# Attention units tied to MLP steps, in a fused attention and ELU-MLP kernel

## The chip, the cores and the metric

One Trainium2 chip, one core. The metric is the device time of one execution in microseconds (us), lower is better. The span of a profile is about 1.8 us shorter than the time of the same execution. A run is classed slow when it is over 1.5% above the fastest of its kernel in its job; ratios use the other runs, called fast, alone. TensorE is called PE in the profile, VectorE DVE, ScalarE ACT, GpSimd POOL, and SP is the engine that issues stores and transposes; PEld is TensorE's weight load.

## The reference, cut to what matters

```python
batch, n_heads, seq, head_dim = (8, 8, 576, 64)      # q, k, v: [8, 8, 576, 64]
q_s = softmax(q over head_dim)                       # exp, divided by its sum
k_s = softmax(k over seq)
kv  = einsum('bhsd,bhse->bhde', k_s, v)              # 64 x 64 per head
att = einsum('bhsd,bhde->bhse', q_s, kv)
x   = att.transpose(0, 2, 1, 3).reshape(4608, 512)
h   = x @ w_in                                       # 512 -> 2048
g   = where(h > 0, h, exp(min(h, 0)) - 1)
out = g @ w_out                                      # 2048 -> 512
```

## The kernel before: the parts that matter

The work is cut in two ways. Attention comes in 16 *units*, each four heads of one batch. The MLP comes in 9 *blocks* of 512 tokens, each of 8 *steps*; a step makes 256 of the 2048 hidden columns. Steps are numbered through: step 8j + g is step g of block j. A program of operations with their reads and writes is built first; a planner then gives each engine its order, by estimated durations, and sets the semaphores. So the order on the chip is fixed beforehand, but each instruction still waits for the real event (in the trace before, VectorE stood 12.6 us at QS, in six waits).

One step (the clamp and the GT tile on VectorE come after each group of eight matmuls):

```python
    def hg(self, j, g, ps, key, how):
        ...   # 8 matmuls 128x128 by 128x512 into the PSUM pair PS[ps]            (line 539)
        ...   # ACT: esb = exp(PS)                                                (line 547)
        # how == "d":
            S.add("dve", ..., e.tensor_scalar(esb, esb, 1.0, -1.0, ALU.min, ALU.add) ...)    # the clamp, line 564
            S.add("dve", ..., e.tensor_tensor(gt, esb, P, ALU.max) ...)                      # GT tile, line 566
        # how == "a": ACT does relu(1 - esb), VectorE one scalar_tensor_tensor (line 560)
```

The attention chain of a unit from 6 on: exp on ScalarE, then sum, reciprocal and QS on VectorE, a transpose by DMA, a widening on GpSimd, the product on TensorE.

```python
        S.add("dve", ..., e.tensor_tensor(qso, q, rz, ALU.mult) ..., W=[f"QS{self.alt(n)}"])   # line 383
    def turn(self, n, key):
        self.S.add("sp", ..., e.dma_start_transpose(self.QT, qs) ..., R=[QS], W=["QT"], dma="tq")
        self.S.ops[-1].packet = 512
    def widen(self, n, key):
        self.S.add("gp", 1200, e.tensor_copy(T, self.QT) ..., R=["QT"], W=[qsT])
```

QS, QT and qsT have one copy each for these units. The planner takes the next operation of an engine that could start first by its estimate. How late a load or transpose is taken to land is set by `margin`:

```python
        S.ops[-1].margin = 300 if n < 4 else self.MARGIN      # MARGIN = 1500 ns; the transposes: 0
        ...
                if x[1] < 1:
                    land[x[2]] = t + 200 + x[2].margin
```

Attention is put into the program as early as its ring of X tiles allows:

```python
        for n in range(4, NU):
            ...
            steps.append([ao(n, 0, merged)] + (more if merged else []))
            steps.append([ao(n, 1)] + ([wide(n + 1)] if nxt else []) + ... +
                         ([first(n + 2), loads(("v", n + 3))] if n + 2 < NU else []))
        def piece(blocks):
            if self.pi < len(steps) and (steps[self.pi][0][0] // 2 + 1) * S_ - RING <= blocks * BLK:
                ...
```

Here `first` is the softmax (and transpose) of a unit, `wide` the widening, `kv` and `ao` its products.

The softmax here doesn't subtract the row's maximum and nothing guards it: scores larger than these inputs give would overflow.

## Time and profile before

| | before |
|---|---|
| time, the three runs at the start | 330.14, 330.22, 337.85 us |
| span of the profiled run (an execution of 328.18 us), granted clock | 326.3 us, 0.989 |
| TensorE busy | 305.5 us (94%) |
| TensorE idle between the first MLP matmul and the tail | 10.6 us |
| VectorE waiting to write QS until a transpose has read it | 12.6 us, 6 times |

How to read it: TensorE at 94% says that it is the bound on the mean, not everywhere. The idle time is length less busy time of each stretch, and the question is what ended each idle stretch. The lines are in the prediction.

### The profile page before, as it was taken

To read this page: it belongs to the slowest core of one execution; us is meant where nothing else is said; L and a number is where in the kernel's file an instruction comes from. 1 tells how busy PE (TensorE), PEld (TensorE's weight loads), DVE (VectorE), ACT (ScalarE), POOL (GpSimd) and SP (SyncE) were. 2 spreads that over 40 slices of the span, in tenths; PEclk is the share of its full clock that TensorE was granted. 3 is DMA by queue.
4 is the path that set the end of the run, shared out by engine and by line. 5 is a ranking of instruction groups with operands and counts; after the bars stand their busy time and mean duration, and the time that the engine had idled before them with its cause. 6 is when DMAs were issued, how large, how long until landed. Compare 5 with 4: busy or idle time off the path is not lost.

```text
span 326.3 us, 4708 instructions
## 1 busy us (share of the span) xinstructions
PE 305.5 (94%) x1997; PEld 239.8 (74%) x1997; DVE 196.4 (60%) x244; ACT 162.7 (50%) x190; POOL 67.2 (21%) x80
## 2 busy tenths in 40 slices
PE   6789999699799989969899999999999999999995
PEld 5577767477477767747678777877788888888873
DVE  4848656967798688376874565454455455545500
ACT  4757668783876554535545442444333333333311
POOL 0760461434453514150420011001000000000000
PEclk9999999899899999999999999999999999999999
DMA  7999998669887864977642162111111111122122
GB/s 271 308 390 390 391 390 327 162 211 169 258 293 181 221 235 93 241 210 145 228 117 57 41 70 66 27 41 32 34 32 32 35 32 32 32 49 50 32 64 65
DMA packets 29525, 49.39 MB, mean 151 GB/s; under 512 B 13888, under 2 KB 13888, under 8 KB 29504
## 3 DMA queue, kind: packets, MB, share of 16 engines
q0 software_dynamic: 10272, 33.16, 33.2%
q1 hardware_dynamic: 19232, 15.93, 21.6%
q8 instruction: 15, 0.25, 0.3%
q14 instruction: 6, 0.05, 0.1%
HBM read 36.70 MB, written 9.44 MB: 141 GB/s over the span
## 4 chain that ended last, share of the span: by engine, by line
PE 74%; DMA 14%; DVE 6%; ACT 2%; POOL 1%; SPq 1%; issue 1%
PE PS L576 35%; PE PS L539 34%; DMA QT<-QS 7%; PE PS L485 3%; DMA QR<-in_q_dram 3%; DMA VR<-in_v_dram 2%; DVE QS L383 2%; DMA W<-in_moe_w_in_dram 2%; DVE ZQ L375 1%; DVE GT L566 1%; PE PS L455 1%; DVE GT L560 1%; POOL qsT L429 1%; ACT QR L359 1%; DVE ESB L564 1%; ACT ESB L547 1%
## 5 line engine op out<-in xcount | busy, mean ns | idle before, releaser
L539 PE MATMUL PS<-XT,W 128*128 128x512 f32 x576 | 146.5, 400 | 4.0 <-DVE GT L560 2.8
L576 PE MATMUL PS<-W,GT 128*128 128x512 f32 x576 | 144.7, 394 | 2.3 <-DVE GT L566 2.3
L539 PEld LDWEIGHTS PS<-XT,W 128*128 128x128 f32 x576 | 108.2, 191 | 29.4 <-DVE GT L560 3.8
L576 PEld LDWEIGHTS PS<-W,GT 128*128 128x128 f32 x576 | 106.7, 188 | 26.6 <-DVE GT L566 3.7
L547 ACT ACTIVATE ESB<-PS 128x1024 f32<-128x1024 f32 x72 | 73.9, 1026 | 92.9 <-PE PS L539 92.9
L564 DVE TENSOR_SCALAR ESB<-ESB 128x1024 f32<-128x1024 f32 x64 | 47.4, 740 | 72.8 <-ACT ESB L547 72.3
L566 DVE TENSOR_TENSOR GT<-ESB,PS 128x1024 fp32r<-128x1024 f32 x64 | 78.2, 1221 | 2.2
L593 ACT ACTIVATE OSB<-PS 128x512 f32<-128x512 f32 x32 | 19.1, 598 | 34.2 <-PE PS L576 34.2
L383 DVE TENSOR_TENSOR QS<-QR,RZQ 128x1152 f16<-128x1152 f32 x16 | 24.1, 1509 | 13.1 <-DMA QT<-QS 12.6
L367 POOL CAST VB<-VR 128x1152 bf16<-128x1152 f32 x15 | 19.6, 1304 | 49.5 <-DMA VR<-in_v_dram 37.7
L375 DVE TENSOR_REDUCE ZQ<-QR 128x18 f32<-128x1152 f32 x16 | 21.6, 1348 | 8.3 <-ACT QR L359 8.2
L507 ACT ACTIVATE XT<-PS 128x640 fp32r<-128x640 f32 (+5 forms) x32 | 19.7, 620 | 13.6 <-PE PS L485 6.8
L359 ACT ACTIVATE QR<-QR 128x1152 f32<-128x1152 f32 x16 | 18.6, 1164 | 11.7 <-DMA QR<-in_q_dram 11.7
L429 POOL CAST qsT<-QT 128x1152 fp32r<-128x1152 f16 x10 | 11.5, 1149 | 62.3 <-PE PS L485 62.3
L485 PE MATMUL PS<-qsT,MBLK 64*128 64x320 f32 (+3 forms) x128 | 17.2, 350 | 5.0 <-DVE MBLK L467 5.0
L485 PEld LDWEIGHTS PS<-qsT,MBLK 64*128 64x128 f32 x128 | 9.7, 188 | 15.5 <-issue 7.4
L362 ACT ACTIVATE KR<-KR 128x1152 bf16<-128x1152 f32 x16 | 18.5, 1162 | 3.0 <-DMA KR<-in_k_dram 3.0
L323 POOL DMA_DIRECT2D QR<-in_q_dram x14 | 10.2, 726 | 24.6 <-DVE QS L383 22.3
L323 POOL DMA_DIRECT2D KR<-in_k_dram x14 | 10.2, 730 | 15.1 <-PE PS L455 15.1
L560 DVE SCALAR_TENSOR_TENSOR GT<-PS,ESB 128x1024 fp32r<-128x1024 f32 x8 | 9.8, 1221 | 5.0 <-ACT ESB L558 5.0
L323 POOL DMA_DIRECT2D VR<-in_v_dram x14 | 10.1, 720 | 2.4 <-POOL VB L367 2.4
L467 DVE TENSOR_SCALAR MBLK<-PS,RZK 128x64 fp32r<-128x64 f32 x32 | 9.1, 284 | 1.1
(28 smaller groups left out, 71.9 us busy)
## 6 DMA issues: line engine op xcount, KB each, us to landing
out_dram<-OSB SPq DMA_DIRECT2D x64, 128.0 KB, 2.3
QR<-in_q_dram POOLq DMA_DIRECT2D x14, 576.0 KB, 6.1
KR<-in_k_dram POOLq DMA_DIRECT2D x14, 576.0 KB, 5.2
VR<-in_v_dram POOLq DMA_DIRECT2D x14, 576.0 KB, 6.1
W<-in_moe_w_in_dram POOLq DMA_DIRECT2D x4, 1024.0 KB, 8.8
W<-in_moe_w_out_dram POOLq DMA_DIRECT2D x4, 1024.0 KB, 18.8
QR<-in_q_dram SPq DMA_DIRECT2D x2, 576.0 KB, 4.1
KR<-in_k_dram SPq DMA_DIRECT2D x2, 576.0 KB, 7.6
```

What stands on the lines that cost most here:

```text
L323: S.add(eng, ISSUE[eng], lambda e: e.dma_start(dst, src), key, W=[name], dma=f"{name}{eng}", nbytes=128 * 4608, follow=self.gpq if chain e ...
L359: S.add("act", t_act(1152, False), lambda e: e.activation(flat(q), flat(q), AF.Exp), key - 3, X=[f"qR{i}"])
L367: S.add(eng, t, lambda e: e.tensor_copy(VB[:, hs, :, 0:D], v[:, hs, :, :]), key - 50, R=[vname], W=[f"VB{i}"])
L375: S.add("dve", t_dve(1152) + 60, lambda e: e.tensor_reduce(self.ZQ[i][:, :, :].rearrange("p h c -> p (h c)"), q[:, :, :, :].rearrange("p h ...
L383: S.add("dve", t_dve(1152) + 60, lambda e: e.tensor_tensor(qso, q[:, :, :, :], rz, ALU.mult), key - 3, R=[f"qR{i}", f"RZQ{i}"], W=[f"QS{se ...
L485: last = e.matmul(P[:, h * 512:h * 512 + n_], M[hs, f, :], T[hs, c0:c1, f * 64:f * 64 + 64], start=(f == 0), stop=(f == 1))
L507: S.add("act", t_act((h1 - h0) * n_, True), lambda e, dst=dst, src=src: e.activation(dst, src, AF.Copy), key, W=W, X=X)
L539: last = e.matmul(P[:, t * 512:(t + 1) * 512], self.W1[:, kc, tt * 128:(tt + 1) * 128], self.XT[:, kc, rc:rc + BLK], start=(kc == 0), stop ...
L547: S.add("act", t_act(1024, True), lambda e: e.activation(esb[:, :], P[:, :], AF.Exp), key, W=[f"E{i}"], X=banks)
L564: S.add("dve", t_dve(1024, 2) + 80, lambda e: e.tensor_scalar(esb[:, :], esb[:, :], 1.0, -1.0, ALU.min, ALU.add), key, X=[f"E{i}"])
L566: S.add("dve", t_dve(1024) + 90, lambda e: e.tensor_tensor(gt, esb[:, :], P[:, :], ALU.max), key, R=[f"E{i}"], W=gw, X=banks)
L576: last = e.matmul(dst, GT[:, jj, ts * 128:(ts + 1) * 128], self.W2[:, jj, :], start=(jj == 0), stop=(jj == 15))
```

## The change

The intent: each stage of units 4 to 15 is tied to a given MLP step, so that the next unit's softmax is not reached while the last one's transpose still runs. An operation made under a gate may not be planned before that step's matmuls start; there is no semaphore for it. Two planning margins rise to 5000 ns. The output matmuls are taken from their list one step later. The keys by which the planner ranks attention work that could start at about the same time (`due`) follow the same table of steps. The diff is cut to these parts.

```diff
@@ one_pass: when may an operation be planned
+            if o.gate is not None:
+                if o.gate.start is None:
+                    return None
+                t = o.gate.start
@@ load, turn
-        S.ops[-1].margin = 300 if n < 4 else self.MARGIN
+        S.ops[-1].margin = 300 if n < 4 else 1500 if n < 6 else 5000
-        self.S.ops[-1].packet = 512
+        self.S.ops[-1].packet, self.S.ops[-1].margin = 512, 5000
@@ program
+        when = {n: (4 * n - 14, 4 * n - 8) for n in range(4, NU)}
+        when.update({4: (8, 9), 5: (10, 12), 6: (12, 16)})
         def due(n):
-            m = n // 2 * S_ // BLK
-            return 12 + 8 * (m - 1) - 9 + 4 * (n % 2)
+            return when[n][1] + 4 if n in when else 3 + 4 * (n % 2)
...
         for n in range(4, NU):
-            (the two steps.append of above)
+            begin, use = when[n]
+            at(begin, first(n), loads(("v", n + 1), ("q", n + 2)))
+            at(use - 2 if n >= BYDMA else use, wide(n))
+            if n == 4:
+                at(use, kv(n), loads(("k", n + 2)))
+            at(use + 1, ao(n, 0))
+            at(use + 2, ao(n, 1, n + 1 if n + 1 < NU else None), loads(("k", n + 3)))
...
+        def paced(s):
+            S.gate = self.last_hg
+            for n, go in slots.pop(s, ()):
+                go()
+            S.gate = None
@@ blocks 2 to 8
-                piece(j)
-                if work[0][0] < j:
+                paced(8 * j + g)
+                if j > 2 or g % 3:
...
+        w = work.pop()
         assert not work
+        self.out_mm(*w, key)
+        self.out_store(w[0], w[1], w[2], key + 1)
```

More of the change, by code (lines that the diff above doesn't have):

```diff
@@ L24 @@
     __slots__ = ("eng", "dur", "emit", "deps", "key", "idx", "start", "end",
-                 "dma", "sem", "val", "clock", "nbytes", "follow", "side", "late", "packet", "margin")
+                 "dma", "sem", "val", "clock", "nbytes", "follow", "side", "late", "packet", "margin",
+                 "gate")
     def __init__(self, eng, dur, emit, key, dma=None, nbytes=0):
@@ L53, in __init__ @@
         self.r = {}
+        self.gate = None
     def add(self, eng, dur, emit, key, R=(), W=(), X=(), dma=None, nbytes=0, after=(),
@@ L58, in add @@
         op.idx = len(self.ops)
-        op.follow, op.side, op.late = follow, side, False
+        op.follow, op.side, op.late, op.gate = follow, side, False, self.gate
         for d in after:
@@ L324, in load @@
               dma=f"{name}{eng}", nbytes=128 * 4608, follow=self.gpq if chain else follow)
-        S.ops[-1].margin = 300 if n < 4 else self.MARGIN
+        S.ops[-1].margin = 300 if n < 4 else 1500 if n < 6 else 5000
         if chain:
             self.gpq = S.ops[-1]
-    MARGIN = 1500
     def raw(self, t, n):
@@ L543, in hg @@
         S.add("pe", 8 * t_f32r(512), mm, key, R=xs + [f"W1_{g // 2}"], X=banks)
+        self.last_hg = S.ops[-1]
         i = self.eslot % len(self.ESB)
@@ L696, in program, with at @@
                  [first(3), loads(("v", 4)), ao(2, 0)], [ao(2, 1), wide(3)],
-                 [kv(3), loads(("q", 5), ("k", 5))], [first(4), loads(("v", 5)), ao(3, 0)],
-                 [ao(3, 1), wide(4)],
-                 [kv(4), loads(("q", 6), ("k", 6)), first(5), loads(("v", 6))]]
+                 [kv(3), loads(("q", 5), ("k", 5)), ao(3, 0)], [ao(3, 1)]]
+        slots = {}
+        def at(s, *what):
+            slots.setdefault(s, []).extend(what)
         for n in range(4, NU):
-            nxt = n + 1 if n + 1 < NU else None
-            merged = nxt if n > 4 else None
-            more = [loads(("k", n + 3), ("q", n + 3))]
-            steps.append([ao(n, 0, merged)] + (more if merged else []))
-            steps.append([ao(n, 1)] + ([wide(n + 1)] if nxt else []) +
-                         ([] if merged or not nxt else [kv(nxt)] + more) +
-                         ([first(n + 2), loads(("v", n + 3))] if n + 2 < NU else []))
-        self.pi = 0
+            begin, use = when[n]
[5 more added lines that the diff above has]
+            at(use + 2, ao(n, 1, n + 1 if n + 1 < NU else None), loads(("k", n + 3)))
         def piece(blocks):
-            if self.pi < len(steps) and (steps[self.pi][0][0] // 2 + 1) * S_ - RING <= blocks * BLK:
-                for n, go in steps[self.pi]:
-                    go()
-                self.pi += 1
+            if steps:
+                for n, go in steps.pop(0):
+                    go()
+        def paced(s):
[3 more added lines that the diff above has]
+            S.gate = None
         key = 0
-        slots = [0, 2, 1]
+        turns = [0, 2, 1]
         for g in range(8):
-            self.hg(0, g, slots[g % 3], key, "da"[g % 2])
+            self.hg(0, g, turns[g % 3], key, "da"[g % 2])
             key += 1
@@ L729, in program @@
             self.out_store(0, ts, (ts + 2) % 4, key)
-        piece(1)
+        while steps:
+            piece(1)
         for g in range(8):
             self.hg(1, g, 2 if g == 0 else g % 2, key, "da"[g % 2])
-            piece(1)
+            paced(8 + g)
             if g >= 2:
```

## The prediction

> **What bounds the kernel now.** I read the page first (busy time and the slices), then a table of busy time by stretch, the TensorE timeline, the chain of work that ended last, and the waits of each engine. From the page, the busy share and the slices of TensorE and its clock:
>
> ```profile
> PE 305.5 (94%) x1997; PEld 239.8 (74%) x1997; DVE 196.4 (60%) x244; ACT 162.7 (50%) x190; POOL 67.2 (21%) x80
> PE   6789999699799989969899999999999999999995
> PEclk9999999899899999999999999999999999999999
> ```
>
> TensorE is the bound, but not all along. From slice 20 on (163 us) it is full; before that some slices show 6 to 8, and two show a lower clock. The table by stretch (length, busy time of PE, PEld, DVE, ACT and POOL, clock, DMA share, GB/s) puts sizes on it:
>
> ```profile
> 52.00:62.70 10.70, 8.03 (x77) 5.94 (x75) 9.60 (x13) 9.34 (x11) 2.58 (x3) 1.00 0.65 205
> 62.70:71.00 8.30, 8.28 (x37) 6.36 (x38) 5.20 (x6) 5.97 (x8) 3.26 (x4) 0.79 0.63 209
> 71.00:86.00 15.00, 12.75 (x126) 9.26 (x124) 12.12 (x17) 9.97 (x12) 5.87 (x7) 1.00 0.99 222
> 107.00:119.30 12.30, 11.05 (x84) 8.47 (x82) 9.60 (x12) 7.33 (x8) 3.98 (x6) 1.00 0.89 257
> 132.50:158.20 25.70, 21.57 (x167) 16.49 (x165) 16.64 (x20) 12.46 (x15) 7.62 (x9) 1.00 0.85 188
> 158.20:190.00 31.80, 31.75 (x177) 25.18 (x178) 20.15 (x25) 14.92 (x18) 4.10 (x4) 1.00 0.34 96
> ```
>
> Length less PE busy gives TensorE's idle time: 2.67, 0.02, 2.25, 1.25, 4.13 and 0.05 us. With 0.20 us in the stretches not shown that is 10.6 us between the first MLP matmul (17.1 us) and the last. After 158 us there is none, although attention work still goes on there until 229 us. What holds TensorE up is in the chain of 132 to 160 us (start, length, what):
>
> ```profile
> 132.33 8.12 DMA QT<-QS
> 140.48 1.36 DVE QS L383
> 141.84 0.09 DVE RZK L464
> ...
> 143.55 1.17 POOL qsT L429
> ...
> 144.73 6.49 DMA QT<-QS
> ...
> 151.25 1.36 DVE QS L383
> ```
>
> and in the timelines of VectorE and TensorE at the same place:
>
> ```profile
> 140.48 1.36 DVE L383 TENSOR_TENSOR QS<-QR,RZQ 128x1152 f16<-128x1152 f32 x1 [4.15 <-DMA QT<-QS]
> 142.61 0.62 PE L485 MATMUL PS<-qsT,MBLK 64*128 64x384 f32 x4 [3.12 <-DVE MBLK L467]
> ```
>
> A unit is four heads of a batch; from unit 6 on its normalized Q (tile QS) is transposed by DMA into QT, and GpSimd widens QT to qsT. QS, QT and qsT each have one copy. With attention issued as early as possible, VectorE reaches the QS of the next unit while the DMA still reads the last one. It stands 4.15 us, and behind it stand MBLK and the MLP's own GT tiles, which TensorE needs. The attention chain (QS, transpose, widen, matmul) is then the bound, not TensorE. The same wait:
>
> ```profile
> DVE QS L383 <- DMA QT<-QS: 12.6, 6, 4.1
> ```
>
> Two groups also ran slow. The eight matmuls from 62.72 us took 3.69 us where the same eight elsewhere take 2.05 after a small attention matmul and 1.81 otherwise, so 1.64 lost; the eight from 86.08 took 3.33, so about 1.3 lost, and a little after. The clock records say the same: 8.3 us x 0.21 = 1.7, and 21 us x 0.08 = 1.7 from 86 to 107. Together 3.3 us.
>
> [...] in those 4.15 us VectorE did none of its other work. [...] the ten transposes took 2.8 to 10.2 us to land (median 4.7) for the same bytes, the long ones among Q, K and V loads. [...] half speed at 62.7 us after a stretch (58.9 to 62.7) with 1.1 us of matmuls, but none after the 3.12 us gap at 142.6.
>
> **The change part by part.** (1) No arithmetic, transfer or byte is added or removed: it is order alone. TensorE's order is the same for both kernels up to the third MLP step of block 1 (51.8 us) and in the last block. So 17.1 us of start, block 0, and 3.9 us from the last matmul to the end stay.
>
> (2) Pacing. One unit per four MLP steps from unit 8 on. A step is 8 + 8 matmuls, 3.63 us; per unit come its two products, 0.49 + 0.43, its KV product, 0.41, and about 2 x 0.24 for the slower matmuls after them: 4 x 3.63 + 1.8 = 16.3 us. The chain from softmax to QS is 1.16 + 1.35 + 0.26 + 1.36 = 4.1 us by the rows of the page's groups, some 6 with the other work of its engines; then the transpose, 4.7 at the median and 10.2 at worst; the widening, 1.15. That is 12 to 17.5 us to the widened tile, which is needed seven steps (28 us) after the beginning; and the next QS is written one period after this one, 16.3 us, more than the 10.2 of the slowest transpose. So the wait on the transpose should go, and with it the idle time at 107 to 119 and 132 to 158: 1.25 + 4.13 = 5.4 us.
>
> (3) Is VectorE able to keep TensorE full? Between two MLP tiles the changed order now puts reduce, reciprocal and QS together, 1.35 + 0.26 + 1.36 = 3.0 us. An MLP tile of VectorE normally ends about 3.2 us after its matmuls (1.03 exp, 0.74, 1.22, hops), and its PSUM tile is reused 5.4 us after them (three groups of 1.81). VectorE has about 1.5 us free in each step, so 3.0 delays a tile by about 1.5 us, less than the 2.2 us of slack. No stall, unless a GpSimd instruction coincides.
>
> (4) Block 1, steps 8 to 15, where units 4 and 5 go by TensorE transposes, and unit 6 starts. I laid the changed order out by hand from 51 us with the durations of the trace, each instruction after its engine's last one and its inputs. Now VectorE does the MLP's tile of step 9 before unit 5's softmax (before: after it, at 61.45 to 62.67), so the fourth step starts at about 59.0 and not 62.7. I then find a 0.4 us wait for MBLK and one of about 1.6 us for the copy of unit 4's first product out of PSUM, behind two MLP instructions on ScalarE (64.8 us); the second product and unit 5's KV product follow, and the fifth step at about 65.8 (before: 67.2). Then no wait up to the second step of block 2, which waits 0.8 us for VectorE and starts at 82.1, where it started at 86.08 with the same matmuls done. So 4.0 us are won there and 2.9 us of idle time stay.
>
> (5) Slow clock. [...] about 1.7 of the 3.3 us stay; I count half, 0.9. The other half was after the idle time at 84 to 86, which goes.
>
> (6) Output tiles lag one step: the last 8 matmuls of a block's outputs move into the next block's first step, and some empty places of block 2 get filled. Same count; they are further from the GT they read. At the end the final 64 output matmuls still follow the last MLP step, so nothing is gained or lost: 0.
>
> Sum: 10.6 + 3.3 = 13.9 us to be had, which would give 330.2 - 13.9 = 316.3. What I expect to stay is 0.4 + 1.6 + 0.8 + 0.9 = 3.7 us. So 330.2 - 10.2 = 320.0 us, or -3.1%.
>
> **Rivals.** A: the transposes are still late. For it: the first paced units (6 and 7) start two steps apart, about 8 us, less than the worst landing, and transposes stand on the same queue as output stores, which wait for ScalarE (159 us of waits there, mostly idle queue). Against it: the stores are now in the same regular order, and loads no longer bunch. One late transpose would cost about 2 to 4 us: 322 to 324. B: pacing pushes attention out to step 54 of 72, so XT could be late for a block's first step. By the ring and the steps, the needed part is done two to three steps ahead (unit 7 at step 21 for block 3 at 24; unit 15 at 53 for block 7 at 56). 8 us of margin speak against it; if wrong, several blocks would each lose some us, and the time is 325 to 335. C: the stalls were hidden anyway and TensorE is equally full: 328 to 331. Against: the idle time is on TensorE itself, which carries 74% of the chain. D: everything goes, 316.3.
>
> **Range and chances.** My value lies 3.7 us above the floor. 316.6 is nearly the floor; 324.2 is the value with one late transpose. 2% faster is 323.6, so I may lose up to half of the gain I count. Faster by over 2%: 0.84; within 2%: 0.14; slower: 0.02.
>
> **What would show it.** Right: the wait of QS for QT near zero; TensorE idle below 0.3 us in 107 to 160; its idle time between the first and last MLP matmul about 3 us rather than 10.6, nearly all before 85 us; attention matmuls regularly spread to some 250 us; full clock after 70 us. Step 3 is wrong if groups of 8 wait for GT in the paced part with no DMA behind it; step 4 if the second step of block 2 does not start 3 to 5 us earlier; step 5 if slow groups remain or new ones come. The whole is wrong if XT or the load of Q, K or V ends TensorE's waits.

## The result, and the profile after

The changed kernel took 319.06 us (median of 4 runs, 317.05 to 321.1) against 330.61 us before (4 runs). The ratio is 0.9655, 95% interval 0.9577 to 0.9734: faster. A ratio here is the mean time of one kernel's fast runs over that of the other's of the same rounds, so it is not quite the ratio of the medians. The predicted 320.0 is 0.9 us off.

The page of the changed kernel, the same three rows:

```profile
PE 305.3 (96%) x1997; PEld 239.8 (76%) x1997; DVE 209.2 (66%) x244; ACT 162.3 (51%) x190; POOL 67.0 (21%) x80
PE   7789999989999999999999999999999999999995
PEclk9979999999999999999999999999999999999999
```

The table by stretch, same stretches (length, busy time of PE, PEld, DVE, ACT and POOL, clock, DMA share, GB/s):

```profile
52.00:62.70 10.70, 10.53 (x54) 8.04 (x53) 8.36 (x10) 9.76 (x12) 1.86 (x2) 1.00 0.71 233
62.70:71.00 8.30, 7.10 (x109) 5.18 (x109) 7.46 (x13) 6.80 (x8) 2.93 (x4) 1.00 0.72 245
71.00:86.00 15.00, 14.72 (x102) 10.82 (x101) 12.48 (x16) 11.75 (x14) 6.30 (x7) 1.00 0.60 192
107.00:119.30 12.30, 12.30 (x57) 9.82 (x56) 8.39 (x10) 6.48 (x8) 4.49 (x5) 1.00 0.95 250
132.50:158.20 25.70, 25.08 (x181) 18.98 (x182) 21.16 (x20) 14.37 (x17) 7.03 (x9) 1.00 0.49 119
```

TensorE's idle time here is 0.17, 1.20, 0.28, 0 and 0.62 us, where it was 2.67, 0.02, 2.25, 1.25 and 4.13. With 0.25 us elsewhere it is 2.5 us instead of 10.6. In this trace VectorE never waits for a transpose any more. TensorE's own list of waits (us in total, times, longest) has, besides those of the start, these lines:

```profile
PE PS L489 <- ACT XT L511: 1.2, 1, 1.2
PE PS L543 <- DVE GT L565: 0.5, 2, 0.3
PE PS L581 <- DVE GT L571: 0.4, 1, 0.4
PE PS L543 <- DVE GT L571: 0.3, 2, 0.2
```

One cost is new. VectorE does the same work as before, but its busy time rose from 196.4 to 209.2 us: the clamps (line 564 before, 569 after) took 740 ns in the mean before and 948 after, 13.3 us in all (w1_widen shows why: 720 there).

The other half of the account is TensorE's clock. The two slow groups of before are gone, but a new one shows at the start. TensorE's timeline, the first 64 MLP matmuls, before and then after:

```profile
17.14 15.00 PE L539 MATMUL PS<-XT,W 128*128 128x512 f32 x64 [1.13 <-DMA W<-in_moe_w_in_dram]
```

```profile
17.31 16.56 PE L543 MATMUL PS<-XT,W 128*128 128x512 f32 x64 [1.10 <-DMA W<-in_moe_w_in_dram]
```

So: 8.1 us less idle time, about 3.3 us of slow matmuls gone, 1.6 us of slow matmuls new, 0.2 us later start: 9.6 us of the 9.1 us by which the span fell from 326.3 to 317.2. The 0.5 us too many lie in TensorE's busy time, which from the first to the last MLP matmul fell by 1.2 us (294.6 to 293.4) and not by 1.7; which matmuls got slower I cannot say.

The slow group at 17 us is not the work of the change: TensorE's order is the same there (up to 51.8 us, as the prediction says), and the trace of b1_qs2, which has the order of the kernel before, shows a low clock there (0.90 at 17 to 34 us, first 64 matmuls in 16.59 us), while that of s7_apart, which is paced, shows none (1.00 at 17 to 23.8 us, 15.06 us). For the clock, one pair of profiles is too little. Each run's record has its granted clock, and (1 - clock) x span is my estimate of what it lost (in the changed kernel's trace 0.005 x 317.2 = 1.6 us, where the slow group lost 1.56; in the one before 0.011 x 326.3 = 3.6, where the slow groups lost about 3.3). Its median in job 2 (see below) is 5.7 us in the eight fast runs of the kernel before, 3.5 in m2_again and 1.6 in a1_again. So up to about 4 of the 10 us between the medians of that job go with the clock, more than the 1.7 of this pair.

### The profile page after: what moved, and what is told of

It reads as the page before. It is cut to its first block, busy times and chain, and to the rows that moved or that the text cites. A ratio compares the mean times of both kernels' runs of the same rounds, so it can differ in the third digit from the quotient of the medians.

```text
span 317.2 us, 4708 instructions
## 1 busy us (share of the span) xinstructions
PE 305.3 (96%) x1997; PEld 239.8 (76%) x1997; DVE 209.2 (66%) x244; ACT 162.3 (51%) x190; POOL 67.0 (21%) x80
## 4 chain that ended last, share of the span: by engine, by line
PE 81%; DVE 7%; ACT 4%; DMA 4%; SPq 0%; issue 0%; POOL 0%
PE PS L581 39%; PE PS L543 38%; PE PS L489 3%; DVE ESB L569 3%; DMA VR<-in_v_dram 2%; DVE GT L571 2%; ACT ESB L552 2%; DMA W<-in_moe_w_in_dram 2%; PE PS L459 1%; ACT ESB L563 1%; DVE QS L387 1%; DVE ZQ L379 1%; SPq L329 0%; ACT XT L511 0%; DVE GT L565 0%
## 5 line engine op out<-in xcount | busy, mean ns | idle before, releaser
L543 PE MATMUL PS<-XT,W 128*128 128x512 f32 x576 | 143.9, 395 | 1.9 <-DMA W<-in_moe_w_in_dram 1.1
L581 PEld LDWEIGHTS PS<-W,GT 128*128 128x128 f32 x576 | 105.6, 188 | 25.5 <-issue 1.9
L569 DVE TENSOR_SCALAR ESB<-ESB 128x1024 f32<-128x1024 f32 x64 | 60.7, 948 | 68.4 <-ACT ESB L552 68.1
L329 POOL DMA_DIRECT2D KR<-in_k_dram x14 | 10.2, 727 | 71.4 <-PE PS L459 71.4
L371 POOL CAST VB<-VR 128x1152 bf16<-128x1152 f32 x15 | 18.5, 1232 | 27.8 <-DMA VR<-in_v_dram 27.8
L387 DVE TENSOR_TENSOR QS<-QR,RZQ 128x1152 f16<-128x1152 f32 x16 | 22.9, 1431 | 0.4
L329 POOL DMA_DIRECT2D VR<-in_v_dram x14 | 10.2, 728 | 3.3 <-POOL VB L371 3.3
```

The costliest lines, as they stand in the source:

```text
L329: S.add(eng, ISSUE[eng], lambda e: e.dma_start(dst, src), key, W=[name], dma=f"{name}{eng}", nbytes=128 * 4608, follow=self.gpq if chain e ...
L387: S.add("dve", t_dve(1152) + 60, lambda e: e.tensor_tensor(qso, q[:, :, :, :], rz, ALU.mult), key - 3, R=[f"qR{i}", f"RZQ{i}"], W=[f"QS{se ...
L543: last = e.matmul(P[:, t * 512:(t + 1) * 512], self.W1[:, kc, tt * 128:(tt + 1) * 128], self.XT[:, kc, rc:rc + BLK], start=(kc == 0), stop ...
L569: S.add("dve", t_dve(1024, 2) + 80, lambda e: e.tensor_scalar(esb[:, :], esb[:, :], 1.0, -1.0, ALU.min, ALU.add), key, X=[f"E{i}"])
L581: last = e.matmul(dst, GT[:, jj, ts * 128:(ts + 1) * 128], self.W2[:, jj, :], start=(jj == 0), stop=(jj == 15))
```

## The experiments

Twelve runs. "Idle" is TensorE's idle time in the profiled run, from about 33 us (the end of block 0's hidden columns) to 300 us; "wait" is what VectorE waited there at QS for QT. The runs of one job share their chip and the runs of the kernel before; the chips differ (before: median 329.23 in job 1, 328.96 in job 2, 326.69 in job 3). The kernel before scatters widely, 323.3 to 338.4 us in 31 runs of job 1; what a ratio there calls its fast runs is its fastest part, so ratios of job 1 flatter the kernel before. So times of different jobs should be compared by their ratios too.

| run | job | median (lowest to highest), runs | ratio, interval | idle | wait |
|---|---|---|---|---|---|
| before, first profile | - | 330.61 (330.14 to 337.85), 4 | 1 | 10.6 | 12.6 |
| changed, first profile | - | 319.06 (317.05 to 321.10), 4 | 0.9655, 0.9577 to 0.9734 | 2.5 | 0 |
| m1_margins | 1 | 322.20 (319.05 to 328.24), 12 | 0.9903, 0.9849 to 0.9957 | 5.0 | 4.6 |
| p2_nomargin | 1 | 326.40 (320.19 to 326.94), 4 | none | 7.9 | 5.8 |
| b1_qs2 | 1 | 326.61 (321.91 to 330.14), 20 | 0.9972, 0.9920 to 1.0024 | 6.8 | 5.1 |
| t1_late2 | 1 | 319.96 (318.04 to 320.85), 4 | 0.9867, 0.9797 to 0.9936 | 3.3 | 0 |
| a1_again | 2 | 318.87 (317.41 to 320.49), 6 | 0.9686, 0.9637 to 0.9735 | 2.5 | 0 |
| m2_again | 2 | 322.22 (320.43 to 324.04), 6 | 0.9804, 0.9751 to 0.9856 | 6.2 | 3.9 |
| s7_apart | 2 | 319.38 (318.02 to 320.91), 6 | 0.9711, 0.9664 to 0.9758 | 3.6 | 0 |
| w1_widen | 2 | 317.11 (315.72 to 318.39), 6 | 0.9642, 0.9594 to 0.9690 | 1.7 | 0 |
| u5_early | 3 | 322.56 (321.84 to 324.82), 4 | 0.9890, 0.9839 to 0.9941 | 7.3 | 4.0 |
| t2_short | 3 | 317.42 (317.04 to 320.47), 4 | 0.9741, 0.9688 to 0.9794 | 4.7 | 1.0 |
| x1_g3d | 3 | 316.67 (315.33 to 318.54), 6 | 0.9703, 0.9658 to 0.9748 | 3.4 | 3.6 |
| x2_spare | 3 | 315.80 (315.64 to 317.10), 6 | 0.9684, 0.9645 to 0.9722 | 2.0 | 1.0 |

The theory (P): pacing takes away the wait of QS for the transpose, and that is the gain. The rivals: the margins do it (M), the output lag does it, or buffers would. The two margins, for loads and for transposes, were only tried together, and the keys of `due` only with the pacing; what each gives by itself is not shown.

**The output lag needed no run.** I put the lag alone into the kernel before, and took it alone out of the changed kernel. In both cases the built program is the same, instruction for instruction and wait for wait, on all five engines. The planner keeps output matmuls in a queue of their own and takes them when TensorE would be free, so their place in the list does not matter here. This part of the change does nothing.

**m1_margins**: the kernel before with the margins alone.

```diff
-        S.ops[-1].margin = 300 if n < 4 else self.MARGIN
+        S.ops[-1].margin = 300 if n < 4 else 1500 if n < 6 else 5000
-        self.S.ops[-1].packet = 512
+        self.S.ops[-1].packet, self.S.ops[-1].margin = 512, 5000
```

> The kernel before, with only the two planning margins of the change (loads of units 6 and later and the transposes are planned to land 5 us later; nothing is tied to a step). Theory P (the gain is the pacing, which keeps one unit per four steps and so takes the wait of QS for the transpose away): the order moves but units still come as early as possible, so TensorE's idle time after 17 us stays above 6 us and the time stays at 326 to 331 us. Rival M (the gain is that the planner knows how late transfers land and puts the MLP's VectorE work ahead of a late QS): at least half of the gain, 319 to 325 us, with the wait of QS for QT below 4 us.

Measured 322.2 us: the time that rival M asked for, not that of P (the wait, 4.6 us, is a little over M's 4). VectorE's wait at QS (us in total, times, longest):

```profile
DVE QS L383 <- DMA QT<-QS: 4.6, 2, 2.8
```

The ratio of this job is unclear by the 2% rule, so it was run again with the changed kernel (there it is 0.9804, again unclear by that rule).

**p2_nomargin**: the changed kernel with the margins put back (1500 and 0).

> The changed kernel without the two planning margins (pacing kept). Theory P: 318 to 322 us, wait of QS for QT below 2 us, because the steps leave more time than a transpose takes. Rival M: 324 us or more, with VectorE or GpSimd waiting several us for QT or for loads.

Four runs: 326.94, 326.08, 326.72, 320.19. Because one is fast, the other three, with the profiled one (clock 0.983), are classed slow, and there is no ratio; so I use no time from it, only the wait that the trace shows; whether the fast run had that wait too is not known. VectorE around the QS of unit 7 (start, length; in brackets the idle time and its cause):

```profile
77.82 1.22 DVE L571 TENSOR_TENSOR GT<-ESB,PS 128x1024 fp32r<-128x1024 f32 x1
84.83 1.36 DVE L387 TENSOR_TENSOR QS<-QR,RZQ 128x1152 f16<-128x1152 f32 x1 [5.79 <-DMA QT<-QS]
86.11 1.22 DVE L565 SCALAR_TENSOR_TENSOR GT<-PS,ESB 128x1024 fp32r<-128x1024 f32 x1
```

The same place in the changed kernel, with the margins:

```profile
77.56 1.22 DVE L571 TENSOR_TENSOR GT<-ESB,PS 128x1024 fp32r<-128x1024 f32 x1
...
81.47 1.23 DVE L565 SCALAR_TENSOR_TENSOR GT<-PS,ESB 128x1024 fp32r<-128x1024 f32 x1 [0.41 <-ACT ESB L563]
...
83.39 1.22 DVE L571 TENSOR_TENSOR GT<-ESB,PS 128x1024 fp32r<-128x1024 f32 x1
84.52 1.35 DVE L387 TENSOR_TENSOR QS<-QR,RZQ 128x1152 f16<-128x1152 f32 x1
```

QS starts at 84.8 in the one and 84.5 in the other. The margin did not make it earlier; it put two MLP tiles ahead of it. Without it they stood behind a transpose that took 11.1 us to land, and TensorE waited 5.0 us for line 565 and then ran one group of eight in 3.78 us. So pacing by itself can leave this wait, and P as I had it falls. Nor do the margins always take it away: x1_g3d below has pacing and both margins, all its runs are fast, and its trace shows a wait of 3.6 us at the same QS.

**s7_apart**: the same without margins, but unit 7 begins four steps after unit 6, as all later units do.

```diff
-        when.update({4: (8, 9), 5: (10, 12), 6: (12, 16)})
+        when.update({4: (8, 9), 5: (10, 12), 6: (12, 16), 7: (16, 20)})
```

> The paced kernel without margins, where VectorE stood 5.8 us at the QS of unit 7 because unit 7 begins two steps (8 us) after unit 6 and the transpose of unit 6 took 11.1 us: now unit 7 begins four steps after unit 6, as all later units do (its use stays). If the close start is the cause, the wait of QS for QT falls from 5.8 to below 1 us, TensorE's 5.0 us wait goes, and the time is 318 to 322 us with no margin at all. If the margins act in another way (order of loads, or other stalls), it stays at 324 to 327 us.

319.38 us, all six runs between 318.0 and 320.9, and no wait of QS for QT at all, though the transpose of unit 6 still took 9.7 us (it landed at 81.9 us, and unit 7's QS began at 83.4). So here the distance of units in steps was enough without margins, once it held for every pair; the margins matter where the change let two units start 8 us apart. The edit also moves the loads that are issued with unit 7's beginning, and that was not tried apart. (TensorE waited 0.7 us for unit 7's widening, the price of the later beginning.)

**a1_again** and **m2_again**: the changed kernel and the margins alone, unedited, in the same rounds.

> The changed kernel once more, unedited, on the same chip and in the same rounds as the next three. Expected 317 to 321 us in every run, with a spread of 4 us [...], against 323 to 338 for the kernel before.

> The kernel before with the two planning margins alone, once more, beside the changed kernel. Theory PM (the gain has two parts that overlap: the margins take the wait at units 6 and 7 away, and pacing takes away the later ones and the stalls of block 1): 320 to 324 us, clearly slower than the changed kernel by 2 to 5 us, with a wider spread because some transposes still come late. Rival M (the margins are the whole gain, pacing adds nothing): within 1 us of the changed kernel.

318.87 against 322.22 us, and the intervals do not overlap. So pacing adds about 3 us to what the margins give. What it adds shows in the idle time at 52 to 63 us: 2.68 us with the margins alone, 0.17 in the changed kernel; the rest is at 71 to 86 (1.80 and 0.29) and 107 to 120 (1.66 and 0). At 120 to 160 us pacing costs 0.80 us, where the margins alone leave none.

**u5_early**: is the early stall the place of unit 5's softmax?

```diff
-        when.update({4: (8, 9), 5: (10, 12), 6: (12, 16)})
+        when.update({4: (8, 9), 5: (8, 12), 6: (12, 16)})
```

> The changed kernel with one number put back towards the old order: unit 5 begins at step 8, not 10. Its softmax then stands ahead of the MLP tile of step 9 on VectorE, as in the kernel before. If that order is the cause of the early stall (2.7 us of idle time at 52 to 63 us in the kernel before, and also with the margins alone, but 0.2 us in the changed kernel), the fourth MLP step of block 1 starts 2 to 4 us later, idle time at 52 to 63 us is 2 to 3 us, a slow-clock window may follow (about 1.5 us), and the time is 321 to 324 us. If the early stall came from loads or transposes, it stays at 317 to 321 us.

322.56 us (its ratio to the kernel before, 0.989, is classed same), and the idle time at 52 to 63 us is back at 2.72 us. Two lines of its VectorE and one of its TensorE:

```profile
59.97 1.36 DVE L387 TENSOR_TENSOR QS<-QR,RZQ 128x1152 f16<-128x1152 f32 x1
61.25 1.22 DVE L565 SCALAR_TENSOR_TENSOR GT<-PS,ESB 128x1024 fp32r<-128x1024 f32 x1
61.39 0.68 PE L410 MATMUL PS<-ID,QS 128*128 128x128 f16 x9 [2.27 <-DVE QS L387]
```

and in the changed kernel the MLP tile comes first:

```profile
59.50 1.22 DVE L565 SCALAR_TENSOR_TENSOR GT<-PS,ESB 128x1024 fp32r<-128x1024 f32 x1 [0.51 <-ACT ESB L563]
...
62.31 1.36 DVE L387 TENSOR_TENSOR QS<-QR,RZQ 128x1152 f16<-128x1152 f32 x1
```

So the early stall has nothing to do with transposes: it is a softmax ahead of an MLP tile. The edit moved more than that, though: later a transpose took 11.5 us and VectorE waited 4.0 us for it, and TensorE idled 3.2 us at 86 to 120. Only the 2.7 us are evidence for the early stall. No low clock followed it at once: the granted clock was 1.00 from 52 to 86 us (0.94 at 86 to 107, 0.96 at 107 to 120).

**b1_qs2**: buffers instead of order. The kernel before, with a second QS for odd units from 7 on; a second QT was in no run, so buffers for the whole chain stay untested. The edit is cut to the new tile.

```diff
+        self.QS.append(a("QS2", [128, CH, 128], F16))      # written and read by odd units from 7 on
```

> The kernel before, unpaced, with a second QS tile for the units of odd number from 7 on, so that the next QS may be written while the last one is still being transposed. Theory P in its narrow form (the loss was VectorE standing at QS behind a transpose, with the MLP's tiles behind it): the wait of QS for QT goes from 12.6 us to below 2 us, TensorE's idle time at 107 to 160 us falls from 5.4 us to below 2 us, and the time to 321 to 326 us without any pacing; the stalls before 86 us stay. Rival Q (the queue is only moved: the next transpose then waits for QT and the widening, attention products come late and TensorE waits for MBLK or qsT instead): 327 to 332 us with new waits of TensorE on MBLK, qsT or XT.

326.61 us, same as before by its interval (the median of all 20 runs is 2.6 us below that of the kernel before). The wait fell only to 5.1 us (three times), since the next transpose itself waits for QT and the widening, and the third QS waits for that: a widening ended at 108.41 us, the next transpose was issued at 108.44, and the QS at 114.30 waited 2.82 us. TensorE's idle time at 107 to 158 us fell from 5.4 to 3.1 us, not below 2. At 107 to 120 us it still stood 2.58 us for a GT tile, in the old way:

```profile
114.30 1.36 DVE L388 TENSOR_TENSOR QS<-QR,RZQ 128x1152 f16<-128x1152 f32 x1 [2.82 <-DMA QT<-QS]
```

```profile
119.23 3.41 PE L581 MATMUL PS<-W,GT 128*128 128x512 f32 x8 [2.58 <-DVE GT L571]
```

One more buffer moved the queue and did not empty it; the rival "the queue is only moved" fits, though the new waits it named on qsT and XT did not come.

**t1_late2**: are the X tiles late? All units from 7 on two steps later.

```diff
-        when = {n: (4 * n - 14, 4 * n - 8) for n in range(4, NU)}
+        when = {n: (4 * n - 12, 4 * n - 6) for n in range(4, NU)}
```

> The changed kernel with every unit from 7 on begun and used two steps later, so that the X tiles of block 3, 4, 5, 6 and 7 are made in the last step before the block that needs them, not three steps before. Theory P with my step on XT (two to three steps of margin, 8 us, are more than needed; one step of 4 us is still enough for a copy of 0.6 to 0.8 us): 318 to 322 us, same as the changed kernel within 1%. Rival B (XT is near its limit): TensorE waits 1 us or more for XT at the start of several blocks, 323 us or more.

319.96 us, about 1 us above the changed kernel's runs (other chips, so no more than an indication; its ratio in job 1, 0.9867, is unclear). TensorE waited once for X, 1.2 us at 111.6 us:

```profile
PE PS L543 <- ACT XT L511: 1.2, 1, 1.2
```

So even one step of lead is enough for all blocks but one, and two to three steps were ample.

**t2_short**: is my chain of 12 to 17.5 us right? Four steps (16 us) instead of seven to the product.

```diff
-        when = {n: (4 * n - 14, 4 * n - 8) for n in range(4, NU)}
+        when = {n: (4 * n - 11, 4 * n - 8) for n in range(4, NU)}
```

> The changed kernel with units from 7 on begun three steps later and used at the same step: four steps (16 us) between the beginning and the first product instead of seven (28 us). My sum said that the chain to the widened tile takes 12 to 17.5 us. So it should just not fit always: TensorE waits for qsT or MBLK several times, 1 to 6 us in total, 319 to 324 us. If the chain were much shorter in the trace, the time stays at 317 to 321 us; if it were longer than 20 us, each of nine units would wait 4 us or more and the time is over 335 us.

One of the units was late:

```profile
104.28 0.66 PE L489 MATMUL PS<-qsT,MBLK 64*128 64x320 f32 x4 [2.85 <-POOL qsT L433]
```

The wait is as expected, the time is not: 317.42 us, below the range. But that range was in the times of other chips. Job 3 ran the kernel before 2.3 us faster than job 2, and by the ratios, 0.9741 here and 0.9686 for the changed kernel in job 2, no gain is shown. The shorter path also moved the widening away from other work on GpSimd (the clamps, 948 ns in the mean in the changed kernel, took 730 here), which may have given back part of what the wait took; the next run shows that effect by itself.

**w1_widen**: the widening one step later.

```diff
-            at(use - 2 if n >= BYDMA else use, wide(n))
+            at(use - 1 if n >= BYDMA else use, wide(n))
```

> The changed kernel with the widening of each unit on GpSimd one step later, so that it no longer runs back to back with the cast of V of the next unit. In the changed kernel the VectorE clamp (128x1024, usually 0.69 us) takes up to 3.83 us when both GpSimd casts fall on it. If that contention is the cause, the clamp's mean falls from 948 ns towards 750 to 820 ns with a maximum near 2 us, and TensorE's idle time at 120 to 160 us from 0.8 to about 0.1 us; time 0 to 1 us better than the changed kernel. If the clamp stays at 3.8 us, the cause is something else [...].

The reason was a line in the changed kernel's VectorE timeline, the clamp of an MLP step, which took 3.81 us where it usually takes 0.69:

```profile
121.58 3.81 DVE L569 TENSOR_SCALAR ESB<-ESB 128x1024 f32<-128x1024 f32 x1
```

GpSimd's timeline at the same time:

```profile
121.89 1.16 POOL L433 CAST qsT<-QT 128x1152 fp32r<-128x1152 f16 x1
122.98 0.70 POOL L329 DMA_DIRECT2D QR<-in_q_dram  x1
123.67 1.16 POOL L371 CAST VB<-VR 128x1152 bf16<-128x1152 f32 x1
```

The clamp ends at 125.39, which is 0.56 us after the second cast. A GpSimd issue alone did not do this: at 104.78 us a clamp took 0.69 us beside one. With the widening one step later, the row of the clamps (count | busy, mean ns), changed kernel and then this one:

```profile
L569 DVE TENSOR_SCALAR ESB<-ESB 128x1024 f32<-128x1024 f32 x64 | 60.7, 948 | 68.4 <-ACT ESB L552 68.1
```

```profile
L569 DVE TENSOR_SCALAR ESB<-ESB 128x1024 f32<-128x1024 f32 x64 | 46.1, 720 | 81.6 <-ACT ESB L552 81.2
```

The longest clamp is 1.54 us, TensorE's idle time at 120 to 160 us is 0 instead of 0.8 us, and the median is 1.8 us below the changed kernel's of the same rounds (317.11 and 318.87). The intervals of the two ratios overlap, so the size is not settled; that the stalls went is.

**x1_g3d** and **x2_spare**: two tries at what is left, on top of w1_widen.

```diff
-            self.hg(1, g, 2 if g == 0 else g % 2, key, "da"[g % 2])
+            self.hg(1, g, 2 if g == 0 else g % 2, key, "d" if g == 3 else "da"[g % 2])
@@ x2_spare: and in the planner's fill, ahead of the first MLP step
+            if o is self.first_hg:
+                p = Op("pe", 16 * 57, self.spare(16), 0)      # 16 matmuls 128x128 of the identity
+                p.start, p.end = o.start, o.start
+                out.append(p)
```

> The later widening (317.1 us) plus the fourth MLP step of block 1 clamped by VectorE instead of ScalarE, which takes 1.06 us off ScalarE ahead of the copy that TensorE waits 1.2 us for. If ScalarE's queue is that wait's cause: the wait falls below 0.4 us and the time to 316 us, within the noise of 1 us. If VectorE becomes the cause instead, a new wait for GT of about 1 us takes its place: no gain.

> The same, with 16 spare 128x128 matmuls on TensorE just before the first MLP step, where it waits 1.0 to 1.5 us for W1 in most runs and then often runs 2 to 4 us at half clock. If the missing activity there is what lowers the clock: the granted clock is 0.995 or more in all runs, the first 64 MLP matmuls take about 15 us (not 16.5 to 17.9), and the time falls by 1 to 2 us, to 314 to 316 us. If the clock does not follow, or the spare matmuls delay the first step: 316 to 318 us.

x1: the wait for the copy went from 1.2 to 0.9 us only, and new waits for GT of 0.9 and 0.8 us came: no gain shown (316.67, another chip). The first of the two has the old cause. The transpose of unit 6 took 11.5 us to land, and VectorE stood at the QS of unit 7, in spite of pacing and margins:

```profile
84.77 1.36 DVE L387 TENSOR_TENSOR QS<-QR,RZQ 128x1152 f16<-128x1152 f32 x1 [3.60 <-DMA QT<-QS]
```

This is rival A of the prediction. In x2 the same wait was 1.0 us. x2 took 315.80 us, four of six runs within 0.2 us of 315.64, the lowest median here; in the same rounds it is 0.9 us below x1. TensorE's timeline at its start:

```profile
16.24 1.07 PE L650 MATMUL PS<-ID 128*128 128x128 f16 x16
17.21 15.02 PE L547 MATMUL PS<-XT,W 128*128 128x512 f32 x64
```

The first 64 matmuls ran at full clock (1.00 at 17 to 25 us). But they did in x1's profile too (14.97 us, without spare matmuls), and in x2's run the clock was low before 13.5 us (0.81 at 6.5 to 10 us, 0.71 at 10 to 13.5), where it cost little: the first MLP matmul began at 17.21 us, 17.31 in the changed kernel (the mean is 0.992, below the 0.995 that I expected). That the spare matmuls keep the clock up is consistent with its narrow spread, and not shown. Which version is best is not shown either: by ratio to the kernel before of the same rounds w1_widen has 0.9642, x2 0.9684 and x1 0.9703, a1_again 0.9686, and the intervals of w1_widen and x2 overlap. x2 has the lowest times, on the fastest of the three chips.

## Why the prediction was right, point by point

**What bounds (right, but incomplete).** TensorE's idle time was the loss, and 8.1 of its 10.6 us went, where I expected 7.8 (10.6 - 2.8; part 4 says 2.9). One reading was too simple. I put the whole 1.25 us at 107 to 119 down to the wait for the transpose; VectorE waited only 0.80 us there, and a reduce of 1.34 us and the small MBLK work also stood ahead of the clamp.

**(1) Order alone: right.** Bytes, instructions and busy time of TensorE (305.5 and 305.3 us) stayed. VectorE's busy time did not: 12.8 us more, for the clamps.

**(2) Pacing takes the wait away: right in the result, wrong in the cause for one pair of units.** The wait went from 12.6 us to none in the profiled run. My argument, one period of 16.3 us against a worst landing of 10.2, holds for units four steps apart. For units 6 and 7, two steps apart, it does not, and without the margins that wait is there (5.8 us in p2_nomargin); even with them it came back in x1_g3d (3.6 us). I had listed it as rival A and gave reasons against it that were not the ones that kept it away. In the changed kernel VectorE reaches unit 7's QS only 10.7 us after unit 6's transpose is issued (73.8 to 84.5 us), so that even a landing of 11.5 us would cost under 1 us; in p2_nomargin it is ready for it after 5.3 us and in x1_g3d, where the planned order is another, after 7.9. My list of parts did not name the margins at all. By themselves they give about 6.7 us of the 10.1 us between the medians of job 2 (328.96 to 322.22 and 318.87). The two remedies overlap: s7_apart has pacing at a distance and no margins, and reaches 319.4.

**(3) VectorE keeps up unless GpSimd coincides: the exception came.** My own sign against this step showed: groups of eight waited for GT with no DMA behind it, and TensorE was idle 0.79 us at 107 to 160, not below 0.3. All of it, 0.17 + 0.62 us at 119 to 158, follows clamps that took up to 3.83 us beside GpSimd's casts. I had named the exception but counted nothing for it, though the trace before has clamps of 1.60 and 1.53 us (at 110.76 and 143.73; median 0.70) beside one GpSimd cast of 1.15 us.

**(4) The hand-laid order of block 1: right.** Predicted: the fourth step at 59.0, the fifth at 65.8, the second step of block 2 at 82.1. Measured: 60.78, 67.07 and 82.75, all behind a start that came 0.17 + 1.56 us later; without this, 59.1, 65.3 and 81.0. The wait for the copy was 1.2 us (I said 1.6), the last one 0.28 (I said 0.8), and the 0.4 for MBLK did not come. u5_early shows the cause, the order on VectorE.

**(5) Slow clock: right in size by luck.** I expected half of the 1.7 us of slow clock near 63 us to stay, 0.9 us; that it would depend on the idle time there was my estimate, and no run shows it. There was no slow clock near 63 us (1.00 at 52 to 86); instead 1.6 us were lost at 17 us, and 2.9 in a1_again (first 64 matmuls in 17.88 us), a term that I did not have and that is not the change's.

**(6) Output lag: zero, right, but my words were wrong.** Nothing moves into the next block and no empty place is filled; the program is the same.

**The sum.** I left 3.7 us above the floor: 0.4 + 1.6 + 0.8 of waits and 0.9 of clock. The profile shows 2.5 us idle and 1.6 us of clock at the start, together 4.1. The base was loose: I took the losses from an execution of 328.18 us and subtracted them from 330.2. From 328.18 the same sum gives 318.0, where the profiled execution after took 318.98.

## What to carry to other kernels

Where one engine serves two chains in an order fixed beforehand, as VectorE does here, look for the instruction that can wait for a slow transfer (VectorE stood 4.15 us at one QS in the trace before, 5.79 in p2_nomargin), and ask what stands behind it: keep its period longer than the slowest landing seen (here a period of 16.3 us, an estimate from the times of part 2, against landings of up to 11.5), or tell the planner the slow landing, so that it puts the bounding engine's work ahead (x1_g3d shows that this does not always suffice). Check the distance of every pair, the first ones too; a rule that holds from the third on leaves its stall at the first. And before reasoning about a part of a change, compare the built programs: a part that a planner undoes costs and gives nothing.

## What else the traces show

- VectorE's clamp beside GpSimd, in the changed kernel's trace (a clamp there takes 0.70 us at the median). Twice it took 3.81 and 3.83 us (at 121.58 and 138.35 us): it ended only after two casts of 1.16 us and the issue of 0.70 or 0.72 us between them. At 155.91 and 172.27 us (2.82 each) it ended 0.7 us after that issue, and the second cast took 1.69 and 1.68 us instead of 1.16. With the widening one step later (w1_widen) the longest was 1.54 us.
- TensorE's clock. The low-clock records of the traces before and after show a clock of 0.50 and last 3.41 us each (apart from those at the end). In the kernel before they start at 62.76 and 86.66 us, 23.89 us or 7 x 3.41 apart; in the changed kernel the one record starts at 17.07 us. In a1_again it was about 6.8 us (an estimate from a clock of 0.95, 0.50 and 0.55 in three stretches of 3.4 us from 13.6 us on). Cut into pieces of 3.41 us from those starts, TensorE was busy 1.15 and 1.08 us in the pieces before the low ones of the kernel before (from 62.76 and 86.66 us), but 2.03 us in the one before that of the changed kernel (from 17.07 us). In the kernel before, pieces with 1.71 us (from 4.74) and 1.64 us (from 137.86; the gap of 3.12 us at 142.6 is split between it and the next) brought no low clock. So busy time in the piece before does not decide by itself, and what does is not shown.
- Landing of the transposes beside other loads. For the same tile (128 x 1152 of 2 bytes) the runs show 2.8 to 11.5 us. The medians of the traces are 4.7 to 7.1. VectorE stood 5.79 and 3.60 us for landings of 11.1 and 11.5 us (p2_nomargin, x1_g3d); at the highest median it would have stood 1.8 us in the one and not at all in the other (an estimate: 7.1 less the 5.3 and 7.9 us after which it was ready).
